# The last two heads' softmax division: the sums carried to the numerators' rows by a 0/1 matmul and inverted there, in place of transposing there and back

## The chip, the cores and the metric

The kernel runs on one core of a Trainium2 chip. The metric is device time in microseconds. Five engines work on it, each in the order of its own queue: TensorE (PE: matmuls, with PEld for its weight loads), VectorE (DVE), ScalarE (ACT), GpSimd (POOL) and SyncE (SP), which issues most DMAs. They wait for each other by semaphores. Matmul results land in PSUM, in eight banks of 128 rows by 512 f32 columns; all else is in SBUF or in DRAM.

## The reference

Two branches share a layer-normalised x (2048 tokens, width 512); their product is added to x:

```
xn = layernorm(x)
q, k, v = split(xn @ wqkv)            # 32 heads of 16
p = softmax(q k^T / 4)                # per head, 2048 x 2048
s = concat_heads(p v) @ wo
h = layernorm(xn)
y = W2 gelu(W1 h + b1) + b2           # over the tokens
out = x + s * silu(y)
```

## The kernel before, in words

**Stages.** First x is normalised and q, k, v are made (to about 147 us). Then one long loop (line 1222) goes over 16 pairs of heads, two spans of 1024 queries for each, and 16 key blocks of 128. For each it computes scores (line 982, 50 rows: 48 of a split q and k, and two rows that subtract the row maximum), the exponential on ACT (line 987), and the values (line 998). Ahead of them the maxima are taken (lines 525 and 529), and the token MLP's matmuls (line 1139) are woven between. When the maxima and the MLP are done, the loop's last part (lines 1273 to 1292) weaves in the output product with wo (lines 1016 to 1024, issued by line 1183, tile dn).

**Values and sums.** The values of a pair of heads go to one PSUM bank of 128 rows by 512 queries, in four strips of 32 rows: head a and query half c make strip 2a + c. v carries 16 columns of ones between the two heads' v, so each strip holds 16 rows of numerators and 16 rows that all equal the softmax sum. For head a = 0 the numerators are rows 0 to 15 of the strip and the sum is row 16; for a = 1 the sum is row 0 and the numerators are rows 16 to 31.

**Division.** `put_away` (line 709) copies the bank to a tile ev. For the first 15 pairs the numerators and sums go to DRAM, are inverted there in a compact shape (line 744: 128 rows of 64 columns) and come back. The last pair has no time for that: `own` (line 812) divides it in SBUF. For each of the two spans:

- `one` transposes ev by 128 columns at a time (line 821: four matmuls with an identity), so that queries are rows and each sum is one column; inverts eight columns twice (line 824); and copies each reciprocal over 32 columns (line 826) to a tile `wide`.
- `two` transposes `wide` back with four f32 matmuls against the identity (line 835, each recorded as two passes), so that every numerator's row has its reciprocal.
- `times` multiplies (line 841, DVE) and makes the upper part of a split number on ACT (line 842); `lower` makes the lower part on DVE (`sub`, line 94).

**Where these run.** The first span's parts are in the list `asides`. In the loop's last part each half-step issues four scores, possibly three matmul items of the output product in two row halves, then one aside (line 1280), then the values that are due. The first span has two asides, `one` and `move_in`; the latter holds `two`, `times`, `lower` and four DMAs on SP that move the 16 numerator rows to their place (line 859). Score tiles and the output product's tiles (dn) take their PSUM banks in turn from one list of seven; the aside's tile takes one from there too.

The second span's parts run after the loop, in the tail (lines 1313 to 1389), which is written out by hand. `some(n)` issues n of 24 matmuls (line 1320) that belong to the last two output blocks and need nothing of the last heads. `product(n)` makes three matmuls (lines 101 to 103) with the last heads' 128 columns k = n // 2: two use the upper part, the third the lower part. `gated`, `added` and `in_parts` (lines 1347 to 1364) multiply a finished block by its gate, add x, and store it. Their DVE work is queued behind that of `times` and `lower`.

Of the kernel before, what the change touches and what calls it, by code (L numbers as in the profile page):

```python
# [8 lines left out]
F32 = mybir.dt.float32  # L9
F32R = mybir.dt.float32r  # L10
AF = mybir.ActivationFunctionType
OP = mybir.AluOpType
# [9 lines left out]
def tile_attention_token_mixer(ctx, tc, x, wqkv, wo, w1, b1, w2, b2, out):  # L22
    nc = tc.nc
    P = 128
    S, D = x.shape
    F = w1.shape[1]
    DH = 16
# [13 lines left out]
    def pool(name, bufs, **kw):  # L41
        return ctx.enter_context(tc.tile_pool(name=name, bufs=bufs, **kw))
# [22 lines left out]
    ps_sc = Banks("ps_sc", 4)  # L65
    ps_mx = Banks("ps_mx", 3)
# [12 lines left out]
    ident = const.tile([P, P], F32, name="ident")  # L79
# [13 lines left out]
    def sub(eng, o, a, b):  # L93
        eng.tensor_tensor(out=o, in0=a, in1=b.bitcast(F32), op=OP.subtract)  # L94

    def move(dst, src, queue=nc.sync):

        queue.dma_start(dst.bitcast(F32), src.bitcast(F32))  # L98
# [7 lines left out]
    qs, ks, vps = {}, {}, {}  # L106
# [63 lines left out]
    with (  # L170
# [15 lines left out]
        for part in range(3):  # L186
            cols = slice(part * D, (part + 1) * D)
# [9 lines left out]
        for n, part in enumerate((2, 0, 1)):  # L197
            for kd in range(ND):
                nm = ("raw", "wh", "wl")[(n * ND + kd) % 3]
# [61 lines left out]
        def first(c, some=range(4)):  # L261
            def dst(b):
                xn[4 * c + b] = px.tile([P, D], F32, name="xn", bufs=8)
                return xn[4 * c + b]

            return Norm(lambda b: xr[4 * c + b], dst, some=some)
# [11 lines left out]
        def bank():  # L278

            i = turn_of[0] = (turn_of[0] + 1) % 8  # L280
            pl, nm = ((ps_sc, "sc"), (ps_mx, "mx"), (ps_av, "av"))[i % 2 if i < 7 else 2]
            return pl.tile([P, 512], F32, name=nm)
# [52 lines left out]
        one, two = first(0, range(2)), first(0, range(2, 4))  # L335
# [65 lines left out]
        for c in range(NC):  # L401
# [20 lines left out]
            for n, (part, g) in enumerate(order):  # L422
                m = slice(g * P, (g + 1) * P)
                begun = c == 0 and part == 0
                ps = pq[g] if begun else bank()
                for w, z in ((wh, 0), (wh, 1), (wl, 0))[begun:]:
                    for kd in range(ND):
                        nc.tensor.matmul(  # L428
                            ps, w[part][:, kd, m], xt[kd][:, z, :],
                            start=w is wh and z == 0 and kd == 0, stop=w is wl and kd == ND - 1,  # L430
# [62 lines left out]
    pp = pool("pp", 18, reuse_waits="tile")  # L493
    sm = pool("sm", 2, reuse_waits="tile")
    el = pool("el", 2, reuse_waits="tile")

    pieces = []
    later = []
# [2 lines left out]
    def after(n, f):  # L501

        later.append(f if n == 1 else lambda: after(n - 1, f))
# [205 lines left out]
    def put_away(p, span, av):  # L709

        ev = el.tile([P, 512], F32, name="ev")
        if p == NP - 1 and span < QH - 1:

            nc.vector.tensor_copy(ev, av)
        else:
            nc.scalar.copy(ev, av)
        if p == NP - 1:
            own(span, ev)
            return
        g, i = divmod(p, 4)  # L720
        if i == 0:
            dens[span] = sm.tile([P, 64], F32, name="d")
        rows = ev.rearrange("(j r) q -> r j q", r=32)
        for a in range(2):
            h = 2 * i + a
            nc.sync.dma_start(
                dens[span][DH * h : DH * (h + 1), :],
                rows[16 - 16 * a, 2 * a : 2 * a + 2, :].rearrange("c (j q) -> c j q", q=64),
            )
        nc.sync.dma_start(num_d[g][span][160 * i : 160 * i + P, :], ev)  # L730
        if i == 3 or p == NP - 2:
            invert(g, span)
# [76 lines left out]
    asides = []  # L809
    own_done = []  # L810

    def own(span, ev):
        rq = sm.tile([P, 4, 4], F32, name="rq", bufs=1)
        wide = el.tile([P, 512], F32, name="t", bufs=4)

        def one(pl=ps_mx, nm="mx", spread=1):

            ps = pl.tile([P, 512], F32, name=nm)
            for k in range(4):
                at = slice(k * P, (k + 1) * P)  # L820
                nc.tensor.transpose(ps[:, at], ev[:, at], ident)
            turned = ps.rearrange("p (k j r) -> p k j r", k=4, j=4)
            for a in range(2):
                nc.vector.reciprocal(rq[:, :, 2 * a : 2 * a + 2], turned[:, :, 2 * a : 2 * a + 2, 16 - 16 * a])
            for k in range(0, 4, 4 // spread):
                nc.vector.tensor_copy(
                    wide.rearrange("p (k j r) -> p k j r", k=4, j=4)[:, k : k + 4 // spread],
                    rq[:, k : k + 4 // spread].unsqueeze(3).to_broadcast([P, 4 // spread, 4, 32]),
                )

        def two(pl=ps_mx, nm="mx", ks=range(4)):

            ps = pl.tile([P, 512], F32, name=nm)
            for k in ks:
                nc.tensor.matmul(
                    ps[:, k * P : (k + 1) * P], wide[:, k * P : (k + 1) * P], ident, start=True, stop=True,
                )
            return ps

        def times(ps, of, at):  # L840
            nc.vector.tensor_tensor(out=ev[:, at], in0=ps[:, at], in1=ev[:, at], op=OP.mult)
            nc.scalar.copy(of[:, 0, at], ev[:, at])

        def lower(of, at):
            sub(nc.vector, of[:, 1, at], ev[:, at], of[:, 0, at])

        if span == QH - 1:
            asides.extend((one, two, times, lower))
            return

        def move_in():
            ps = two()
            of = el.tile([P, 2, 512], F32R, name="uo")
            times(ps, of, slice(0, 512))
            lower(of, slice(0, 512))
            for a in range(2):
                for c in range(2):
                    row = 32 * (2 * a + c) + DH * a
                    move(oc[ND - 1, c][96 + DH * a : 112 + DH * a, :, :], of[row : row + DH, :, :])
            after(4, lambda: own_done.append(True))  # L860

        asides.extend((one, move_in))


    last_w = {}
# [77 lines left out]
    def plan_halves():  # L943

        rows = [oc[g, c][:, m, :].bitcast(F32) for c in range(NC - 1) for g in range(ND - 1) for m in range(2)]
        own = PARTS - NB // 2
        for n in range(own, len(blocks) - 3):
            b = blocks[n]
            in_halves.extend(((ys, b, y_d[b]), (gts, b, g_d[b])))
        in_halves.extend((gates, b, g_d[b]) for b in range(NB // 2, NB))  # L950
        in_halves[:] = [(to, b, row, of) for (to, b, of), row in zip(in_halves, rows, strict=True)]
# [175 lines left out]
    def halves(lead, n):  # L1127


        parts, then = ([], []), []  # L1130

        def each(x, f):
            if f:
                then.append(f)
                return
            ps, w, m, first, last = x
            for a, made in ((lead, parts[0]), (1 - lead, parts[1])):
                r = slice(64 * a, 64 * a + 64)
                made.append(lambda r=r, start=first and a == lead, stop=last and a != lead: nc.tensor.matmul(  # L1139
                    ps, w(r), m(r), start=start, stop=stop,  # L1140
                ))

        take(n, each)
        return *parts, then
# [5 lines left out]
    def count():  # L1150


        left = -done
        for i, n in enumerate(sizes):
            left += n
            if left > 0:
                break
        new_block[0] = left == n
        if left == 9:
            return 4  # L1160
        return min(6, -(-left // -(-3 * left // (15 if i == SLOW else 16)))) if left > 0 else 0
# [60 lines left out]
    for s in range(0, total + 1, 2):  # L1222
# [13 lines left out]
        if s < NU and t >= 0:  # L1236
            steady[0] = True
            one, two, then = halves(lead, count())
# [18 lines left out]
        elif s < NU:  # L1257

            for i in range(4):
# [4 lines left out]
                some = []  # L1264
# [35 lines left out]
        if 0 <= t < NT:  # L1300
            p, r = divmod(t, SPP)
# [13 lines left out]
    for b in range(PARTS, NB):  # L1315
        sums[b] = ps_sc.hold("dn")[0][:, :D]
        for g in range(ND):
            o, at = oc[g, b // 4], slice(b % 4 * P, (b % 4 + 1) * P)
# [5 lines left out]
    def some(n):  # L1324
        for f in beside[:n]:
            f()
        del beside[:n]

    one, two, times, lower = asides
    some(4)  # L1330
    one(ps_sc, "sc", 4)
    some(3)
    shares = [two(ps_sc, "sc", [k]) for k in range(4)]
    some(1)
    of = ks[NP - 1][:, :1024].rearrange("p (a q) -> p a q", a=2)
    half = [NB // 2 + 4 * c + k for k in range(4) for c in range(2)]
# [27 lines left out]
            nc.sync.dma_start(out[b * P : (b + 1) * P, at], to[:, at])  # L1364


    cols = [slice(k * P, (k + 1) * P) for k in range(4)]
    for k in range(5):
        if k < 4:
            times(shares[k], of, cols[k])  # L1370
# [46 lines left out]
```

## Time and profile before

| | |
|---|---|
| median of the runs | 1627.11 us |
| fastest run | 1627.04 us |
| the profiled execution's own time | 1627.03 us |
| its span, first to last instruction | 1625.2 us |
| granted TensorE clock | 1.00 |

In the profile, each row of a timeline has the start in us from the span's beginning, the duration, the engine, the line of the kernel, the operation, out<-in tiles with their shapes, and in brackets how long the engine stood idle before and who released it. Rows that follow each other on one engine and are alike are merged, with their count. Rows of groups have count, busy us, mean ns of one, and idle us before.

### The profile page before, as it was taken

The numbers are of one execution on the slowest core, as the hardware profiler recorded it, in microseconds if no ns is written. First come the engines' busy times: TensorE is split into PE (matmuls) and PEld (weight loads), VectorE is DVE, ScalarE is ACT, GpSimd is POOL, SyncE is SP. The second block draws the span as 40 slices with busy tenths as digits, with TensorE's granted clock in tenths as the row PEclk, the third lists the DMA queues.
The fourth block names the chain that finished last, engine by engine and source line by source line (L and its number), as shares of the span: only waits on it lengthen the run. The fifth ranks groups of instructions, "written<-read, shape, count | busy, mean of one in ns | idle before, by whom it ended". The sixth has DMA issues, their size and how long they took to land.

```text
span 1625.2 us, 31294 instructions
## 1 busy us (share of the span) xinstructions
PE 1618.5 (100%) x11956; PEld 880.1 (54%) x11956; DVE 1422.0 (87%) x2500; ACT 1195.7 (74%) x2313; POOL 559.5 (34%) x663
## 2 busy tenths in 40 slices
PE   9999999999999999999999999999999999999998
PEld 7888854554555544544545545444555455444444
DVE  7655999999999999999999999999999999999956
ACT  3333477777777777778877877777778778888885
POOL 1224844342244432342333332322322224632440
PEclk9999999999999999999999999999999999999999
DMA  7478441515143141826151512314151615453364
GB/s 227 175 248 210 114 94 41 95 41 76 41 70 72 32 80 34 244 67 109 40 86 38 94 56 41 79 23 68 37 86 38 112 39 94 121 102 118 112 203 176
DMA packets 152466, 155.60 MB, mean 96 GB/s; under 512 B 51628, under 2 KB 110252, under 8 KB 149244
## 3 DMA queue, kind: packets, MB, share of 16 engines
q1 hardware_dynamic: 147900, 152.85, 38.6%
q8 instruction: 94, 1.54, 0.4%
q0 software_dynamic: 4416, 0.75, 0.4%
q14 instruction: 56, 0.46, 0.1%
HBM read 101.86 MB, written 50.58 MB: 94 GB/s over the span
## 4 chain that ended last, share of the span: by engine, by line
PE 99%; DVE 1%; ACT 0%; DMA 0%; issue 0%; DVEq 0%
PE av L998 31%; PE dn L1139 25%; PE sc L982 17%; PE mx L525 14%; PE dn L663 3%; PE sc L428 3%; PE mx L428 2%; PE av L428 1%; PE sc L101 0%; PE sc L103 0%; PE sc L102 0%; PE mx L982 0%; PE dn L1320 0%; PE mx L101 0%; PE mx L103 0%; PE mx L102 0%
## 5 line engine op out<-in xcount | busy, mean ns | idle before, releaser
L529 DVE TENSOR_REDUCE mxp<-mx 128x1 f32<-128x512 f32 x2026 | 1250.8, 682 | 117.4 <-PE mx L525 92.2
L987 ACT ACTIVATE prob<-sc 128x512 f32<-128x512 f32 x2004 | 1039.1, 606 | 282.9 <-PE sc L982 127.8
L525 PE MATMUL mx<-big 48*128 48x512 f32 x2026 | 773.0, 418 | 0.0
L982 PE MATMUL sc<-big 50*128 50x512 f32 x2004 | 738.5, 412 | 0.1
L998 PE MATMUL av<-prob,vp 128*32 128x512 f32 x4096 | 545.5, 604 | 0.0
L1139 PE MATMUL dn<-hu,wh 64*128 64x512 f32 x1520 | 508.0, 404 | 0.0
L982 PEld LDWEIGHTS sc<-big 50*128 50x128 f32 x2004 | 354.4, 186 | 234.5 <-ACT prob L987 210.4
L525 PEld LDWEIGHTS mx<-big 48*128 48x128 f32 x2026 | 358.0, 185 | 196.3 <-DVE mxp L529 177.9
L1139 PEld LDWEIGHTS dn<-hu,wh 64*128 64x128 f32 x1520 | 271.7, 184 | 75.2 <-issue 49.5
L1139 PE MATMUL dn<-hu,wl 64*128 64x512 f32 x762 | 302.0, 396 | 0.0
L998 PEld LDWEIGHTS av<-prob,vp 128*32 128x32 f32 x4096 | 80.9, 108 | 178.0 <-issue 166.1
L94 POOL TENSOR_TENSOR wl<-raw,wh 128x512 fp32r<-128x512 f32 x124 | 150.9, 1219 | 60.3 <-ACT wh L166 27.0
L1139 PEld LDWEIGHTS dn<-hu,wl 64*128 64x128 f32 x762 | 140.5, 184 | 13.3
L164 POOL CAST wh<-raw 128x512 fp32r<-128x512 f32 x104 | 60.5, 582 | 189.3 <-PE sc L982 54.4
L552 POOL CAST m<-f 16x128 fp32r<-16x128 f32 x32 | 9.0, 281 | 304.7 <-DVE f L541 304.7
L98 POOL DMA_DIRECT2D big<-m x128 | 66.4, 527 | 2.7 <-PE mx L982 2.7
L613 POOL TENSOR_TENSOR sq<-u 128x512 f32<-128x512 f32 x11 | 11.5, 1042 | 132.7 <-ACT u L607 132.6
L1139 PE MATMUL dn<-wh,hu 64*128 64x512 f32 x168 | 55.0, 392 | 0.0
L700 POOL TENSOR_SCALAR t<-t 128x512 f32<-128x512 f32 x16 | 23.8, 1490 | 83.5 <-ACT t L697 83.5
L428 PE MATMUL sc<-xt,big 128*128 128x512 f32 x184 | 44.5, 390 | 0.0
L94 POOL TENSOR_TENSOR hu<-hx,hu 128x512 fp32r<-128x512 f32 x16 | 20.4, 1296 | 68.5 <-ACT hu L271 68.5
L663 PE MATMUL dn<-hu,wh 64*128 64x512 f32 x128 | 42.3, 391 | 0.0
(231 smaller groups left out, 1216.2 us busy)
## 6 DMA issues: line engine op xcount, KB each, us to landing
raw<-in_B_w_dram SPq DMA_DIRECT2D x104, 256.0 KB
big<-k_d SPq DMA_DIRECT2D x96, 128.0 KB
big<-q_d SPq DMA_DIRECT2D x96, 128.0 KB
q_d<-sg SPq DMA_DIRECT2D x16, 512.0 KB
k_d<-sg SPq DMA_DIRECT2D x16, 512.0 KB
num_d<-ev SPq DMA_DIRECT2D x30, 256.0 KB
u_d<-uo SPq DMA_DIRECT2D x14, 512.0 KB
hu<-u_d SPq DMA_DIRECT2D x14, 512.0 KB
```

The source lines that it names most:

```text
L94: eng.tensor_tensor(out=o, in0=a, in1=b.bitcast(F32), op=OP.subtract)
L98: queue.dma_start(dst.bitcast(F32), src.bitcast(F32))
L164: nc.gpsimd.tensor_copy(whs[n][:, :m, :], raws[n][:, :m, :])
L428: nc.tensor.matmul(ps, w[part][:, kd, m], xt[kd][:, z, :], start=w is wh and z == 0 and kd == 0, stop=w is wl and kd == ND - 1,)
L525: nc.tensor.matmul(ps, q[o : o + 48, r * P : (r + 1) * P], k[o : o + 48, c * 512 : (c + 1) * 512], start=True, stop=True,)
L529: nc.vector.tensor_reduce(mxp[u // 16][:, a, r % 8, c : c + 1], ps, axis=AX.X, op=OP.max)
L663: nc.tensor.matmul(ps, w(slice(0, 64)), m(slice(0, 64)), start=first, stop=last)
L700: nc.gpsimd.tensor_scalar(t, t, 1.0, None, op0=OP.add)
L982: nc.tensor.matmul(ps, ks[p][o : o + 50, kb * P : (kb + 1) * P], qs[p][o : o + 50, at : at + 512], start=True, stop=True,)
L987: nc.scalar.activation(e, ps, AF.Exp, scale=scale)
L998: nc.tensor.matmul(av[32 * j : 32 * j + 32, :], vps[p][:, kb, 16 * a : 16 * a + 32], prob.pop((t, a, c)), start=kb == 0, stop=kb == NB - 1,)
L1139: made.append(lambda r=r, start=first and a == lead, stop=last and a != lead: nc.tensor.matmul(ps, w(r), m(r), start=start, stop=stop,))
```

## The change

A tile `pick` (128 by 128, f32) is made once from the identity by four POOL copies. Its columns 32j to 32j + 31 are all the identity's column of the row that holds strip j's sum, so the matmul of `pick` with ev puts, in all 32 rows of each strip, that strip's sum. `one` and `two` become one function `share`, a single f32 matmul over the columns asked for, with `pick` as weights. The reciprocal is taken in `times`, of all 128 rows and all columns, from PSUM to `wide`. The first span's asides become one (`move_in`). In the tail there are four shares of 128 columns, each in a bank of its own, directly behind `some(4)`; `some(3)` between the transposes is gone, and these three matmuls are issued later by the `some` ahead of block 14.

```
+    pick = sm.tile([P, P], F32, name="pick", bufs=1)
+    for j in range(4):
+        row = 32 * j + (DH if j < 2 else 0)
+        nc.gpsimd.tensor_copy(pick[:, 32 * j : 32 * j + 32], ident[:, row : row + 1].to_broadcast([P, 32]))
...
     def own(span, ev):
-        rq = sm.tile([P, 4, 4], F32, name="rq", bufs=1)
         wide = el.tile([P, 512], F32, name="t", bufs=4)

-        def one(pl=ps_mx, nm="mx", spread=1):
+        def share(pl=ps_mx, nm="mx", at=slice(0, 512)):

             ps = pl.tile([P, 512], F32, name=nm)
-            for k in range(4):
-                at = slice(k * P, (k + 1) * P)
-                nc.tensor.transpose(ps[:, at], ev[:, at], ident)
...
-        def two(pl=ps_mx, nm="mx", ks=range(4)):
-
-            ps = pl.tile([P, 512], F32, name=nm)
-            for k in ks:
-                nc.tensor.matmul(
-                    ps[:, k * P : (k + 1) * P], wide[:, k * P : (k + 1) * P], ident, start=True, stop=True,
-                )
+            nc.tensor.matmul(ps[:, at], pick, ev[:, at], start=True, stop=True)
             return ps

         def times(ps, of, at):
-            nc.vector.tensor_tensor(out=ev[:, at], in0=ps[:, at], in1=ev[:, at], op=OP.mult)
+            nc.vector.reciprocal(wide[:, at], ps[:, at])
+            nc.vector.tensor_tensor(out=ev[:, at], in0=wide[:, at], in1=ev[:, at], op=OP.mult)
             nc.scalar.copy(of[:, 0, at], ev[:, at])
...
         if span == QH - 1:
-            asides.extend((one, two, times, lower))
+            asides.extend((share, times, lower))
             return

         def move_in():
-            ps = two()
+            ps = share()
             of = el.tile([P, 2, 512], F32R, name="uo")
             times(ps, of, slice(0, 512))
             lower(of, slice(0, 512))
...
-        asides.extend((one, move_in))
+        asides.append(move_in)
...
-    one, two, times, lower = asides
+    share, times, lower = asides
+    cols = [slice(k * P, (k + 1) * P) for k in range(4)]
     some(4)
-    one(ps_sc, "sc", 4)
-    some(3)
-    shares = [two(ps_sc, "sc", [k]) for k in range(4)]
+    shares = [share(ps_sc, "sc", at) for at in cols]
     some(1)
```

More of the change, by code (lines that the diff above doesn't have):

```diff
@@ L812, in own @@
     def own(span, ev):
-        rq = sm.tile([P, 4, 4], F32, name="rq", bufs=1)
         wide = el.tile([P, 512], F32, name="t", bufs=4)
-        def one(pl=ps_mx, nm="mx", spread=1):
+        def share(pl=ps_mx, nm="mx", at=slice(0, 512)):
             ps = pl.tile([P, 512], F32, name=nm)
-            for k in range(4):
-                at = slice(k * P, (k + 1) * P)
[L821 to L828, printed above, removed]
-                )
-        def two(pl=ps_mx, nm="mx", ks=range(4)):
-            ps = pl.tile([P, 512], F32, name=nm)
-            for k in ks:
-                nc.tensor.matmul(
-                    ps[:, k * P : (k + 1) * P], wide[:, k * P : (k + 1) * P], ident, start=True, stop=True,
-                )
+            nc.tensor.matmul(ps[:, at], pick, ev[:, at], start=True, stop=True)
             return ps
         def times(ps, of, at):
-            nc.vector.tensor_tensor(out=ev[:, at], in0=ps[:, at], in1=ev[:, at], op=OP.mult)
+            nc.vector.reciprocal(wide[:, at], ps[:, at])
+            nc.vector.tensor_tensor(out=ev[:, at], in0=wide[:, at], in1=ev[:, at], op=OP.mult)
             nc.scalar.copy(of[:, 0, at], ev[:, at])
@@ L1364, in in_parts @@
             nc.sync.dma_start(out[b * P : (b + 1) * P, at], to[:, at])
-    cols = [slice(k * P, (k + 1) * P) for k in range(4)]
     for k in range(5):
```

## The prediction

> **What bounds the kernel now.** I read the page first (span, engines, chain), then the timeline of the two places where the last heads are divided, then the DVE groups by shape for reciprocals.
>
> ```profile
> span 1625.2 us, 31294 instructions
> PE 1618.5 (100%) x11956; PEld 880.1 (54%) x11956; DVE 1422.0 (87%) x2500; ACT 1195.7 (74%) x2313; POOL 559.5 (34%) x663
> PE 99%; DVE 1%; ACT 0%; DMA 0%; issue 0%; DVEq 0%
> ```
>
> TensorE (PE) is the bound throughout: 99% of the chain that ended last, the other 1% being DVE at the very end. So a pass less on PE is worth its pitch, and a new wait of PE is lost whole. The change touches two places: the first span's division, beside scores and values ("the middle"), and the second span's, on the way to the last products ("the tail"). The middle, before:
>
> ```profile
> 1571.04 0.50 PE L982 MATMUL sc<-big 50*128 50x512 f32 x1
> ...
> 1571.20 0.69 DVE L714 COPY ev<-av 128x512 f32<-128x512 f32 x1
> ...
> 1572.04 0.63 PE L821 MATMUL mx<-ident,ev 128*128 128x128 f32 x4 [0.27 <-DVE ev L714]
> ...
> 1572.60 1.07 PE L998 MATMUL av<-prob,vp 128*32 128x512 f32 x8
> ...
> 1573.08 0.62 ACT L987 ACTIVATE prob<-mx 128x512 f32<-128x512 f32 x1
> ...
> 1573.60 0.50 PE L982 MATMUL sc<-big 50*128 50x512 f32 x1
> ...
> 1574.13 1.09 ACT L987 ACTIVATE prob<-sc 128x512 f32<-128x512 f32 x2 [0.43 <-PE dn L1183]
> ...
> 1574.60 0.69 DVE L962 TENSOR_TENSOR sq<-dn,sq 128x512 f32<-128x512 f32 x1 [1.16 <-PE dn L1183]
> ...
> 1574.96 1.16 PE L835 MATMUL mx<-ident,t 128*128 128x128 f32 x8
> ...
> 1576.05 1.07 PE L998 MATMUL av<-prob,vp 128*32 128x512 f32 x8
> ...
> 1576.15 0.69 DVE L841 TENSOR_TENSOR ev<-mx,ev 128x512 f32<-128x512 f32 x1
> 1576.88 0.62 ACT L842 CAST uo<-ev 128x512 fp32r<-128x512 f32 x1 [0.69 <-DVE ev L841]
> ...
> 1577.04 0.50 PE L982 MATMUL sc<-big 50*128 50x512 f32 x1
> ...
> 1577.70 1.06 PE L998 MATMUL av<-prob,vp 128*32 128x512 f32 x8
> ...
> 1578.25 2.53 SPq L98 DMA_DIRECT2D hu<-uo  x4
> ...
> 1578.70 0.50 PE L982 MATMUL sc<-big 50*128 50x512 f32 x1
> ...
> 1581.06 0.50 PE L982 MATMUL sc<-big 50*128 50x512 f32 x1
> ```
>
> The columns are start, duration, engine, line, operation and tiles. The PE rows of scores mark half-steps, which I call H0 (from 1571.04), H1 (1573.60), H2 (1577.04), H3 (1578.70). A half-step has four scores and eight value passes; H1 and H3 have six matmuls of the output product (dn) too. Without an aside a half-step lasts 1.66 (H2: 1578.70 - 1577.04) or 2.36 (H3: 1581.06 - 1578.70). H0 lasts 2.56 and H1 3.44, so the two asides cost PE 0.90 + 1.08 = 1.98 us. ACT is nearly as full: its exponentials follow each other every 0.49 us (two in 1.09 with 0.60 each), eight of them 3.9 us in the 4.02 us of two half-steps, and the values of a half-step need the four exponentials of the half-step before.
>
> **The price on which it hangs** is a reciprocal of 128 or 512 columns, which the kernel before never runs:
>
> ```profile
> L744 DVE RECIPROCAL d<-d 128x64 f32<-128x64 f32 x6 | 3.3, 553 | 0.2
> L239 DVE RECIPROCAL r<-t 128x4 f32<-128x4 f32 x7 | 1.2, 178 | 1.9 <-ACT t L234 1.9
> L239 DVE RECIPROCAL r<-t 128x2 f32<-128x2 f32 x2 | 0.3, 160 | 0.3 <-ACT t L234 0.3
> L824 DVE RECIPROCAL rq<-mx 128x8 f32<-128x8 f32 x2 | 0.3, 182 | 0.8 <-PE mx L821 0.8
> ```
>
> From 4 to 64 columns it grows by (553 - 178)/60 = 6.25 ns a column over 153 ns fixed; 2 columns (165 worked out, 160 seen) fit. The row from PSUM, 8 columns in 182, gives 203 by that line, so a PSUM source is not dearer per column. Estimates: 128 columns 0.95 us, 512 columns 3.35 us. Bounds: all of the 553 in the columns, 8.64 ns each, gives 1.11 and 4.42; below, the multiplications of the same shapes, 0.28 and 0.69, if a long run went at their rate. I take the line, since 64 columns lie nearest to it.
> [...]
>
> **The middle, step by step.** Removed from PE: four transposes and eight passes. Added: one f32 product of 512 columns. Eight value passes, which are four strips of such a product side by side, take 1.00 (1577.70 to the next PE row, 1578.70), eight passes over 128 columns 1.09 (1574.96 to 1576.05); I take 1.0. It starts at 1572.04 as the transposes did (it waits for the same copy, L714), so it ends at 1573.04 where the transposes let the values start at 1572.60: 0.44 later. H1 then has no aside (1.08 gone): H2 would start at 1576.40 and not 1577.04, 0.64 us gained, if nothing waited.
> But it waits. The two asides are now one, so the upper part's copy stands on ACT behind H0's four exponentials and ahead of H1's four. DVE: product seen at about 1573.15 (transposes 1572.67 to reciprocal 1572.71 shows the gap), reciprocal to 1576.50, multiplication 0.69 to 1577.23, ACT's copy 0.62 to 1577.89. H1's exponentials, which ran from 1574.13, start about 1577.77 (0.5 behind the copy's start) and end at 1578.37, 1578.86, 1579.33, 1579.82. ACT had been free since 1573.70 (1573.08 + 0.62).
> PE meanwhile goes through H1 (its values need only H0's exponentials) to 1576.40. H2's first score takes the bank that the reciprocal read: 1576.55. The second and third take banks of H1's first and second scores: 1578.4 and 1578.9. The fourth takes the bank of the dn block whose evacuation (L962, before at 1574.60) is now queued on DVE behind the reciprocal, the multiplication and the lower part, which itself waits for the copy: lower part 1577.93 to 1578.62, evacuation to about 1579.25, score at 1579.3. H2's values end with the strip that needs the fourth exponential: 1579.86 + 1.0 = about 1580.8. H3 started at 1578.70 before, so the middle costs **+2.1 us** net. H2's exponentials end by 1581.75, H3's values want them at 1582.2: no further wait. PE is full from there, so none of the 2.1 comes back.
> On SP the four moves of uo (1578.25 before, about 1578.65 after) now stand ahead of four loads that were issued before them. These loads' tiles are used by later output blocks, 10 us on; cost nothing, at most the 2.5 us that the moves take to issue, if that cover were gone.
>
> **The tail, step by step,** in the clock of before, the 2.1 left out:
>
> ```profile
> 1608.68 0.60 PE L821 MATMUL sc<-ident,ev 128*128 128x128 f32 x4
> ...
> 1609.32 0.28 DVE L824 RECIPROCAL rq<-sc 128x8 f32<-128x8 f32 x2 [2.94 <-PE sc L821]
> ...
> 1609.91 1.16 PE L835 MATMUL sc<-ident,t 128*128 128x128 f32 x8
> 1610.51 0.49 DVE L841 TENSOR_TENSOR ev<-sc,ev 128x128 f32<-128x128 f32 x2 [0.24 <-PE sc L835]
> ...
> 1610.84 0.30 ACT L842 CAST big<-ev 128x128 fp32r<-128x128 f32 x1 [2.49 <-DVE ev L841]
> ...
> 1611.19 0.51 PE L101 MATMUL sc<-uo,big 128*128 128x512 f32 x1
> ...
> 1612.63 1.28 DVE L1351 TENSOR_TENSOR prob<-sc,hu 128x512 f32<-128x512 f32 x2
> ...
> 1614.43 1.49 DVE L1355 TENSOR_TENSOR prob<-big,prob 128x512 f32<-128x512 f32 x2
> ...
> 1615.85 1.87 DVE L1351 TENSOR_TENSOR prob<-sc,hu 128x512 f32<-128x512 f32 x3
> ...
> 1617.64 1.47 DVE L1355 TENSOR_TENSOR prob<-big,prob 128x512 f32<-128x512 f32 x2
> ...
> 1619.04 0.68 DVE L1351 TENSOR_TENSOR prob<-dn,hu 128x512 f32<-128x512 f32 x1
> ...
> 1619.75 0.69 DVE L1355 TENSOR_TENSOR prob<-big,prob 128x512 f32<-128x512 f32 x1
> ...
> 1620.30 0.39 PE L103 MATMUL dn<-uo,big 128*128 128x512 f32 x1
> 1620.73 0.42 DVE L1362 TENSOR_TENSOR prob<-dn,hu 128x256 f32<-128x256 f32 x1 [0.29 <-PE dn L103]
> ```
>
> PE: the four share products start at 1608.68 (0.27 each, the rate of L835: 1.09 for four), one dn matmul follows, to 1610.0. The first reciprocal starts at 1609.28 (L835 to L841 shows 0.60 from first pass to reader). DVE then runs, for each of four columns, reciprocal 0.95 + 0.04, multiplication and lower part at 0.21 each (the pitch of L841's pair): reciprocals start at 1609.28, 1610.48, 1611.89, 1613.30, the last lower part about 1614.95. DVE comes to its first gating at 1615.17; before, at 1612.63.
> PE's first product wants ACT's copy (1610.85): 1610.9, 0.3 earlier than 1611.19, but its third matmul wants the first lower part, which stands on DVE behind two reciprocals: 1611.96, a wait of 0.6. Three dn matmuls that filled the gap before stand later, so 43 matmuls follow against 40 before, at 0.2336 (39 pitches from 1611.19 to 1620.30): the last starts at 1621.3 and not 1620.30. **PE alone: +1.0.**
> DVE's work behind the lower parts takes, by the starts above, 1.80 for three gatings, 1.42 for two sums (1614.43 to 1615.85), 1.79, 1.40, 0.71, and 0.65 for the last sum: 7.8 us with no wait left in it. 1615.17 + 7.8 = 1622.95 for L1362, at 1620.73 before; PE is done by then. **The tail costs +2.2**: DVE is the bound there, and PE's +1.0 lies beside it.
>
> **The mask.** Four POOL copies to fill pick wait for a late matmul of the V product:
>
> ```profile
> 145.90 0.39 PE L103 MATMUL mx<-wvh,xt 128*128 128x512 f32 x1
> ...
> 148.20 1.28 POOL L94 TENSOR_TENSOR wl<-raw,wh 128x512 fp32r<-128x512 f32 x1 [4.35 <-ACT wh L166]
> ...
> L552 POOL CAST m<-f 16x128 fp32r<-16x128 f32 x32 | 9.0, 281 | 304.7 <-DVE f L541 304.7
> ```
>
> That matmul ends at 146.29. The smallest POOL cast seen takes 0.28, so four copies end by about 147.4; POOL waits for ACT until 148.20. Nothing, or up to 1 us if they took longer, held up the weight split, and the first blocks wanted it.
>
> **Sum.** 2.1 + 2.2 = +4.3 us. The profiled execution took 1627.03 us (span 1625.2, 1.8 around it), the median shown is 1627.11: 1627.1 + 4.3 = **1631.4 us**.
>
> **Rivals.**
> - *The reciprocal is dearer:* 8.64 ns a column. Middle +1.07 more, tail 4 x 0.15 more: +6.0, 1633.1. The fixed time of the short reciprocals speaks against it. [...]
> - *The middle's wait is absorbed,* because another strip order or a spare bank lets PE run on: only the tail, and between -0.64 and 0 in the middle: 1628.7 to 1629.3. For it: ACT stood 0.69 for L841 before and PE lost nothing. Against: 3.6 us is more than a half-step of 2.0.
> - *Not slower:* a long reciprocal runs at the rate of other DVE work (0.69 and 0.28). Then the copy ends near 1575.2, H2 waits only some 0.15, middle about -0.5; in the tail the first product starts at 1610.25 without a gap: -0.24. 1626.4. It decides where 512 columns take under some 1.3 us; the 553 for 64 columns is against it.
>
> **Numbers.** Forecast 60%, dearer reciprocal 14%, middle absorbed 14%, not slower 7%, something else 5%. The forecast's own range is 1630.2 to 1632.6 (the f32 product between 0.9 and 1.1, the waits 0.5 either way). With the two neighbours the range is 1628.4 to 1634.0. All cases lie within 2%, about what a measurement of this kernel can tell from no change (1594.6 to 1659.7): same 98%; slower by over 2% 1.5%, faster 0.5%, both only through something not seen here.
>
> **What would show it.** L826 in the changed kernel: reciprocals of 128x512 near 3.35 us and of 128x128 near 0.95. ACT's copy after a gap of 3.5 us behind H0's exponentials; H2 about 4 us long in place of 1.66. In the tail, DVE without idle from the first reciprocal to the last block and PE done before it. I am wrong if the 128x512 reciprocal is under 2 us, or if PE's half-steps show no stretch.

## The result, and the profile after

The changed kernel takes 1633.22 us (median of 6 runs, 1631.15 to 1634.63); the kernel before takes 1627.06 beside it (6 runs). One of these six took 3885.2 us, the other five 1626.84 to 1627.11. The ratio is 1.0036 with the 95% interval [1.0025, 1.0047]: 6.2 us slower, within 2%, with an interval that excludes no change. The forecast was +4.3 (1631.4). The sign, the two places and the price of each held; a third loss of some 1.5 to 1.7 us was not in the sum.

The profiled run of the changed kernel took 1632.96 us, with a span of 1631.1; the span before was 1625.2. The unseen price comes first. These are the reciprocals of the changed kernel in the groups by shape (count, busy us, mean ns of one, idle before):

```profile
L826 DVE RECIPROCAL t<-sc 128x128 f32<-128x128 f32 x4 | 3.8, 952 | 2.7 <-PE sc L822 2.7
L826 DVE RECIPROCAL t<-mx 128x512 f32<-128x512 f32 x1 | 3.4, 3357 | 1.3 <-PE mx L822 1.3
L748 DVE RECIPROCAL d<-d 128x64 f32<-128x64 f32 x6 | 3.3, 553 | 0.2
```

The line through 4 and 64 columns gave 0.95 and 3.35 us; 952 and 3357 ns were measured. The upper bound of 8.64 ns a column, 1.11 and 4.42 us, isn't borne out: the two rows differ by 2405 ns over 384 columns, 6.26 ns each.

Now the middle of the changed kernel, in the timeline (start, duration, engine, line, operation and tiles, and in brackets the idle time before and its releaser). H0 starts at 1571.20 here:

```profile
1571.20 0.50 PE L968 MATMUL sc<-big 50*128 50x512 f32 x1
...
1572.20 1.10 PE L822 MATMUL mx<-ev,pick 128*128 128x512 f32 x2 [0.27 <-DVE ev L718]
...
1573.33 3.36 DVE L826 RECIPROCAL t<-mx 128x512 f32<-128x512 f32 x1 [1.28 <-PE mx L822]
...
1574.79 0.40 PE L1169 MATMUL dn<-wh,hu 64*128 64x512 f32 x2
...
1576.72 0.69 DVE L827 TENSOR_TENSOR ev<-t,ev 128x512 f32<-128x512 f32 x1
1576.74 0.50 PE L968 MATMUL sc<-big 50*128 50x512 f32 x1
1577.45 0.62 ACT L828 CAST uo<-ev 128x512 fp32r<-128x512 f32 x1 [3.59 <-DVE ev L827]
1577.97 1.08 ACT L973 ACTIVATE prob<-sc 128x512 f32<-128x512 f32 x2
1578.10 0.69 DVE L94 TENSOR_TENSOR uo<-ev,uo 128x512 fp32r<-128x512 f32 x1 [0.68 <-ACT uo L828]
1578.62 0.50 PE L968 MATMUL mx<-big 50*128 50x512 f32 x1 [1.37 <-ACT prob L973]
1578.71 0.69 DVE L948 TENSOR_TENSOR sq<-dn,sq 128x512 f32<-128x512 f32 x1
...
1579.88 1.39 PE L984 MATMUL av<-prob,vp 128*32 128x512 f32 x8
...
1581.20 0.79 PE L968 MATMUL sc<-big 50*128 50x512 f32 x1
...
1582.22 0.63 PE L1169 MATMUL dn<-wh,hu 64*128 64x512 f32 x2
...
1583.63 1.36 PE L984 MATMUL av<-prob,vp 128*32 128x512 f32 x8
...
1584.91 0.50 PE L968 MATMUL sc<-big 50*128 50x512 f32 x1
```

The reader is to see three things. ACT stood idle for 3.59 us, until the multiplication gave it its copy, and H1's exponentials start only behind that copy (1577.97). PE, after one score of H2 at 1576.74, stands for 1.37 until the first of them has freed a bank. And from about 1580.9 on PE's own rows are longer: eight value passes take 1.39 and 1.36 where they took 1.06 (the 1.39 is in part a wait, as an experiment below shows), and the dn matmuls of 1582.22 take 0.63, with the next 0.42 behind them, where those of H1 (1574.79) took 0.40 with the next 0.23 behind. The longer dn matmuls are no wait: it is the clock. The windows show it (busy us of PE, PEld, DVE, ACT and POOL with their counts, then the granted clock, the DMA share and GB/s), before first and the changed kernel second:

```profile
1576.00:1586.00 10.00, 10.00 (x76) 3.88 (x75) 4.18 (x7) 9.19 (x19) 0.00 (x0) 1.00 0.63 176
```

```profile
1576.00:1586.00 10.00, 8.54 (x46) 3.16 (x42) 4.75 (x7) 7.20 (x14) 0.00 (x0) 0.83 0.48 134
```

A granted clock of 0.83 over 10 us is 1.7 us of full clock lost. In windows of 0.25 us it is 1.00 up to 1580.75, 0.73 in the next, 0.50 from 1581.00 to 1584.25, 0.95 in the next and then 1.00 again: half the clock for 3.4 us, from about 1580.87 to 1584.28. From H0 to the half-step behind H3 it takes 13.71 us (1571.20 to 1584.91), where it took 10.02 (1571.04 to 1581.06): +3.7, of which at most 1.7 is the clock, so that at least 2.0 is the wait.

The tail of the changed kernel:

```profile
1611.51 0.50 PE L1306 MATMUL dn<-wh,hu 128*128 128x512 f32 x1
...
1612.96 0.96 DVE L826 RECIPROCAL t<-sc 128x128 f32<-128x128 f32 x1 [2.71 <-PE sc L822]
...
1614.70 0.50 PE L101 MATMUL sc<-uo,big 128*128 128x512 f32 x1 [0.87 <-ACT big L828]
...
1615.76 0.50 PE L103 MATMUL sc<-uo,big 128*128 128x512 f32 x1 [0.33 <-DVE big L94]
...
1618.66 0.29 DVE L94 TENSOR_TENSOR big<-ev,big 128x128 fp32r<-128x128 f32 x1 [0.16 <-ACT big L828]
```

```profile
1624.97 0.39 PE L103 MATMUL dn<-uo,big 128*128 128x512 f32 x1
```

```profile
1626.58 0.41 DVE L1347 TENSOR_TENSOR prob<-dn,hu 128x256 f32<-128x256 f32 x1
```

I measure the tail from the first of the `some(4)` matmuls (1611.51; 1607.65 before) to the last block's multiplication (L1347 here, L1362 before). It takes 15.07 us; before it took 13.08 (1607.65 to 1620.73): +2.0. From the reciprocal on DVE has one gap, of 0.16. L1347 has no bracket: it waited for nobody, while its like before waited 0.29 for PE. PE's last matmul starts 13.46 behind the first, before 12.65: +0.8, beside DVE's time as forecast.

### The profile page after: what moved, and what is told of

It reads as the page before. It is cut to its first block, busy times and chain, and to the rows that moved or that the text cites. A ratio compares the mean times of both kernels' runs of the same rounds, so it can differ in the third digit from the quotient of the medians.

```text
span 1631.1 us, 31263 instructions
## 1 busy us (share of the span) xinstructions
PE 1620.9 (99%) x11942; PEld 880.4 (54%) x11942; DVE 1427.0 (87%) x2496; ACT 1196.0 (73%) x2313; POOL 559.7 (34%) x667
## 4 chain that ended last, share of the span: by engine, by line
PE 98%; DVE 1%; ACT 0%; issue 0%; DMA 0%; POOL 0%; DVEq 0%; POOLq 0%
PE av L984 31%; PE dn L1125 24%; PE sc L968 16%; PE mx L529 14%; PE sc L428 3%; PE dn L667 2%; PE mx L428 2%; PE av L428 1%; PE mx L332 0%; PE sc L103 0%; PE sc L101 0%; PE sc L102 0%; PE dn L1169 0%; PE dn L668 0%; PE mx L103 0%; PE mx L101 0%
```

## The experiments

The theory: DVE's reciprocal delays two chains of the middle (about +2.0), PE's wait there lets the granted clock fall (about +1.7, not forecast), and DVE sets the end of the tail (+2.0). Against it stand the rivals that the reciprocal isn't the cause at all but the new order of the asides, that the slow rows come from the matmul with `pick` and not from the wait, and that the tail's loss is PE's. The kernels have other line numbers; tiles and operations tell the rows. Times are medians, with the kernel before on the same chip.

**One part at a time.** The middle changed and the tail as before:

```
-    share, times, lower = asides
+    one, two, times, lower = asides
...
-    shares = [share(ps_sc, "sc", at) for at in cols]
+    one(ps_sc, "sc", 4)
+    some(3)
+    shares = [two(ps_sc, "sc", [k]) for k in range(4)]
```

> The first span is divided as in the changed kernel, the second span as before. Theory (the reciprocal's columns cost the time; the middle and the tail add up; the wait in the middle also drops TensorE's clock): about +2.2 us with a clock of 1.000 and up to +5.7 where the clock drops after the wait, so 1629.3 to 1632.8, with a spread of some us between runs. Rival (the clock drop has nothing to do with the middle): 1629.3 in every run, clock 1.000. Rival (the middle's wait is given back later): 1627.

And the tail changed, with the middle as before:

```
         def move_in():
-            ps = share()
+            ps = two()
...
-            times(ps, of, slice(0, 512))
+            times_back(ps, of, slice(0, 512))
...
-        asides.append(move_in)
+        asides.extend((one, move_in))
```

> The first span is divided as before, the second span as in the changed kernel. Theory: +2.0 us, 1629.1, no spread, clock 1.000 in every run, because no PE wait is long enough here to move the clock. Rival (the clock drop comes with the change as a whole, or at random): a spread of some us as in the changed kernel. Rival (PE, not DVE, bounds the tail): +0.8, 1627.9.

Before took 1626.75. The middle alone took 1630.56 (+3.8, ratio 1.0024 [1.0014, 1.0033]), from 1628.83 to 1631.50; the tail alone 1628.85 (+2.1, ratio 1.0014 [1.0004, 1.0024]). The fastest run of the middle alone, with a granted clock of 1.000 over the run, is 2.1 above before. Its profiled run (clock 0.998) again has slow PE rows, between 1579.76 and 1583.52, and 0.83 granted over 1576 to 1586. The tail alone has 1.00 there, its runs lie between 1628.03 and 1629.63, about as wide as those of before (1626.19 to 1628.16), and their clocks are 0.999 or 1.000, as those of before are. So the fall belongs to the middle.

**Is it the reciprocal?** The same order of work with a copy in its place, which leaves the inversion out (the numerators are multiplied by the sums):

```
-            nc.vector.reciprocal(wide[:, at], ps[:, at])
+            nc.vector.tensor_copy(wide[:, at], ps[:, at])
```

> The changed kernel with copies in place of its five wide reciprocals, so that the inversion is left out and the numerators are multiplied by the sums. Theory (it is the reciprocal's 6.25 ns a column): a copy takes 0.69 or 0.28 us, nothing waits long, the PE work saved shows: 1626.4, clock 1.000. Rival (the order of the queues costs the time, whatever stands in the reciprocal's place): 1629 or more.

It took 1626.14 (-0.6, ratio 0.9998 [0.9988, 1.0007], not clear of noise).

```profile
1574.80 0.69 DVE L826 COPY t<-mx 128x512 f32<-128x512 f32 x1 [1.28 <-PE mx L822]
```

The copy takes 0.69 for 512 columns, and H3 starts 7.20 after H0 (1572.66 to 1579.86) against 7.66 before: -0.46. The clock is 1.00 over 1576 to 1586 with the same matmul with `pick` in place, so that matmul doesn't make the slow rows. The share matmul and the single aside cost nothing by themselves: in this order of work the whole loss comes with the reciprocal's length. It is also the rival "not slower" run as a kernel: -0.5 in the middle and 1626.4 were worked out for it.

**Is it the wait that lowers the clock?** The changed kernel, with 20 transposes of the identity put ahead of H2's first score, where PE has next to nothing to do:

```
+        if filler[0] == 1:
+            for _ in range(20):
+                nc.tensor.transpose(ps[:, :P], ident, ident)
+            filler[0] = 0
```

> The changed kernel with 20 transposes of the identity ahead of the first score that waits in the middle, about 1.8 us of work inside the 2 us wait; their results are overwritten. Theory (the wait itself lets TensorE's clock fall, and that is the rest of the loss): clock 1.000 in every run, time 1631.2 without the spread of the changed kernel (1631.15 to 1634.63). Rival (the clock has another cause): the same spread, median 1633; and where the filler does not fit into the wait, up to 1.8 us more.

Its PE rows:

```profile
1571.53 0.50 PE L974 MATMUL sc<-big 50*128 50x512 f32 x1
...
1577.08 2.40 PE L972 MATMUL sc<-ident 128*128 128x128 f32 x20
1579.41 0.50 PE L974 MATMUL sc<-big 50*128 50x512 f32 x1
...
1580.22 1.25 PE L990 MATMUL av<-prob,vp 128*32 128x512 f32 x8
...
1581.40 0.50 PE L974 MATMUL sc<-big 50*128 50x512 f32 x1
...
1582.77 1.07 PE L990 MATMUL av<-prob,vp 128*32 128x512 f32 x8
1583.77 0.50 PE L974 MATMUL sc<-big 50*128 50x512 f32 x1
```

With more work on PE it is faster: 1631.18 (7 runs, 1630.31 to 1631.81), +4.4 beside its own runs of before (ratio 1.0027 [1.0016, 1.0038]), where the changed kernel was +6.2 beside its own. Its clocks are 0.999 or 1.000 in all runs. From H0 (1571.53) to the half-step behind H3 it takes 12.24, +2.2 over before and 1.5 less than the changed kernel; H3's values take 1.07, and the windows show 1.00 over 1576 to 1586. The transposes take 2.33 and not the 1.8 expected, but they delay nothing: H2's values start 8.69 behind H0, in the changed kernel 8.68 (1579.88). So the wait is as long as ever, but filled, and the fall is gone. Held at full clock, the 3.7 of the middle split into 2.2 for the wait and 1.5 for the clock. That is less than the 1.7 of lost clock, for H2's values take 1.25 here too: part of their 1.39 in the changed kernel was not the clock's. What the spread of the changed kernel is made of fits: its fastest run, 1631.15, had a clock of 1.000 over the run and lies 4.1 above before; the other five had 0.997 or 0.998 and took 1632.29 to 1634.63. There is a trace of the profiled run alone, so that the fall is missing in the fastest is inferred from its clock.

**Which chain does PE wait for?** Three versions of the middle, tail as before, and the changed kernel again beside them. In the changed kernel ACT's copy delays the exponentials, and the dn evacuation (DVE reading a finished dn block out of its PSUM bank, which frees the bank for a score) is queued on DVE behind the lower part. First, the copy moved to POOL, so that ACT is free:

```
-            times(ps, of, slice(0, 512))
+            nc.vector.reciprocal(wide, ps)
+            nc.vector.tensor_tensor(out=ev, in0=wide, in1=ev, op=OP.mult)
+            nc.gpsimd.tensor_copy(of[:, 0, :], ev)
```

> The middle as changed, the tail as before; in the middle the upper part's copy runs on POOL, so ACT's exponentials no longer stand behind it, while on DVE the lower part still stands ahead of the dn block's evacuation. Theory (two chains of about the same length, over ACT and over DVE, end the same wait): the fourth score still waits for the evacuation, some 1.8 us net in place of 2.2: only 0.3 to 0.4 us better than middle only. Rival (it is ACT's queue alone): the whole wait goes, 1626.5.

Second, ACT's copy left where it was, and the lower part and the moves put into one aside later, so that DVE's queue is free for the evacuation:

```
+        def divide_it():
+            ps = share()
+            now_of.append(el.tile([P, 2, 512], F32R, name="uo"))
+            times(ps, now_of[0], slice(0, 512))
+
         def move_in():
-            ps = share()
-            of = el.tile([P, 2, 512], F32R, name="uo")
-            times(ps, of, slice(0, 512))
+            of = now_of[0]
             lower(of, slice(0, 512))
...
-        asides.append(move_in)
+        asides.extend((divide_it, move_in))
```

> The middle as changed, the tail as before; in the middle the lower part and the moves come one aside later, so that the dn block's evacuation stands ahead of the lower part on DVE, while ACT's copy stays where it was. Theory (two chains): H2's second score still waits for the first exponential behind the copy, 2.1 to 2.2 us net, no gain against middle only. Rival (it is DVE's queue alone): the wait goes, 1627 or less.

Third, both: the first aside is the share and the reciprocal, the second the multiplication, with both parts on POOL:

```
+        def invert_it():
+            nc.vector.reciprocal(wide, share())
+
         def move_in():
-            ps = share()
...
-            times(ps, of, slice(0, 512))
-            lower(of, slice(0, 512))
+            nc.vector.tensor_tensor(out=ev, in0=wide, in1=ev, op=OP.mult)
+            nc.gpsimd.tensor_copy(of[:, 0, :], ev)
+            sub(nc.gpsimd, of[:, 1, :], ev, of[:, 0, :])
...
-        asides.append(move_in)
+        asides.extend((invert_it, move_in))
```

> The middle's first aside is the sums' matmul and the reciprocal alone; the multiplication comes one aside later, and both parts are made on POOL; the tail as before. Both queues are freed, the reciprocal is the same 3.36 us. Theory: the evacuation waits only for the reciprocal (some 0.3 us on H2's fourth score), ACT for nothing, the PE work saved shows: -0.2 to -0.4 against before, 1626.5, clock 1.000. Rival (DVE held for 3.4 us costs by itself): 1628 or more.

> The changed kernel once more, on the chip of the runs beside it. Theory (the middle +2.2, the tail +2.0, the clock's fall 0 to 3.5): 1631 to 1634.6 with a spread of over 2 us, on a chip whose runs of before are at 1626.8.

Before took 1627.43 here. The changed kernel took 1634.12 (4 runs, ratio 1.0039 [1.0024, 1.0054]). These medians hold the clock's fall too, where a run has it. ACT freed alone took 1630.56 (+3.1, ratio 1.0018 [1.0008, 1.0027]), DVE's queue freed alone 1630.85 (+3.4, 1.0020 [1.0010, 1.0029]), both 1627.17 (-0.3, 0.9998 [0.9989, 1.0008], no difference clear of noise). The rows say why one is not enough. With ACT free:

```profile
1577.70 0.50 PE L1000 MATMUL sc<-big 50*128 50x512 f32 x1
...
1579.08 0.69 DVE L94 TENSOR_TENSOR uo<-ev,uo 128x512 fp32r<-128x512 f32 x1 [0.71 <-POOL uo L872]
...
1579.69 0.69 DVE L980 TENSOR_TENSOR sq<-dn,sq 128x512 f32<-128x512 f32 x1
...
1580.43 0.56 PE L1000 MATMUL mx<-big 50*128 50x512 f32 x1 [2.00 <-DVE sq L980]
```

three scores of H2 go at once, and the fourth waits 2.00 us for the bank of the dn block, whose evacuation stands on DVE behind the lower part. With DVE's queue free:

```profile
1577.60 0.69 DVE L983 TENSOR_TENSOR sq<-dn,sq 128x512 f32<-128x512 f32 x1
1577.72 0.62 ACT L858 CAST uo<-ev 128x512 fp32r<-128x512 f32 x1 [3.60 <-DVE ev L857]
1578.24 1.08 ACT L1008 ACTIVATE prob<-sc 128x512 f32<-128x512 f32 x2
...
1578.88 0.49 PE L1003 MATMUL mx<-big 50*128 50x512 f32 x1 [1.37 <-ACT prob L1008]
```

the evacuation comes early, and PE stands for ACT as it did. With either wait the clock is 0.83 over 1576 to 1586. With both freed:

```profile
1573.32 3.36 DVE L868 RECIPROCAL t<-mx 128x512 f32<-128x512 f32 x1 [1.28 <-PE mx L852]
...
1576.60 0.63 DVE L981 TENSOR_TENSOR sq<-dn,sq 128x512 f32<-128x512 f32 x1
...
1577.28 0.49 PE L1001 MATMUL mx<-big 50*128 50x512 f32 x1
...
1578.70 0.49 PE L1001 MATMUL sc<-big 50*128 50x512 f32 x1
```

the same 3.36 us reciprocal runs, the fourth score comes 0.54 after the first (1576.74), and H3 starts 7.51 behind H0 (1571.19), 0.15 sooner than before, at a clock of 1.00. The matmul with `pick` is in it too. Here the long reciprocal costs nothing by its length; in the changed kernel it costs by what was queued behind it.

**The tail: DVE or PE?** With the middle as before, the tail's lower parts were moved to POOL, and then each reciprocal of the tail taken twice:

```
-            sub(nc.vector, of[:, 1, at], ev[:, at], of[:, 0, at])
+            sub(nc.gpsimd if span == QH - 1 else nc.vector, of[:, 1, at], ev[:, at], of[:, 0, at])
```

> As the run with only the tail changed (the middle is that of before), and the four lower parts of the tail are made by POOL, not by DVE. Theory (DVE without idle sets the end, PE's later end lies beside it): DVE loses four times 0.21 us, so the tail costs +2.1 - 0.84 = about +1.3, about 1628.0 beside 1626.7; the last block's multiplication still has no wait for PE ahead of it. POOL's subtraction of 128 columns should take about 0.35 (it took 1.29 for 512 columns beside 0.69 on DVE), so the first product's third matmul waits less than 0.33. Rival (the tail's cost is PE's: the wait of 0.33 for the first lower part, the 0.87 ahead of the first product, and three matmuls that stand later): the end follows PE, which gains only the wait, so +1.8 to +2.1 is left.

```
             nc.vector.reciprocal(wide[:, at], ps[:, at])
+            nc.vector.reciprocal(wide[:, at], ps[:, at])
```

> As the run with only the tail changed (the middle is that of before), and each of the tail's four reciprocals is taken twice. Theory: DVE runs without idle, so four more of 0.95 + 0.04 come straight on top: +2.1 + 4.0 = about +6.1, about 1632.8 beside 1626.7, and DVE shows no idle time from the first reciprocal to the last block. Rival (PE sets the end): only what stands ahead of the first product counts: one reciprocal more ahead of the first upper part, two ahead of the first lower part, so +2.1 + 1.0 to 2.0 = +3.1 to +4.1, with idle time on DVE ahead of the last block.

Before took 1626.87. Lower parts on POOL: 1627.72 (+0.9, ratio 1.0006 [0.9997, 1.0016], not clear of noise, +1.3 expected); reciprocals twice: 1632.75 (+5.9, ratio 1.0037 [1.0023, 1.0051]). The traces are sharper than the medians. The last block's multiplication, in the one and in the other, waits for nobody:

```profile
1621.05 0.42 DVE L1377 TENSOR_TENSOR prob<-dn,hu 128x256 f32<-128x256 f32 x1
```

```profile
1626.47 0.42 DVE L1378 TENSOR_TENSOR prob<-dn,hu 128x256 f32<-128x256 f32 x1
```

From the first `some(4)` matmul to the last block's multiplication the first takes 14.04 (1607.01 to 1621.05) and the second 19.03 (1607.44 to 1626.47), against 13.08 before and 15.09 with the tail alone (1607.16 to 1622.25). Taking 4 x 0.21 and the gap of 0.17 from DVE shortens the tail by 1.05, and adding 4 x 0.99 lengthens it by 3.94: DVE sets it. One POOL subtraction took 0.45, not the 0.35 I had expected, and that cost nothing.

The doubled tail shows the clock a second time (the last row is of the windows):

```profile
1611.62 0.50 PE L101 MATMUL sc<-uo,big 128*128 128x512 f32 x1 [1.86 <-ACT big L859]
1611.96 0.39 PE L102 MATMUL sc<-uo,big 128*128 128x512 f32 x1
1613.68 0.80 PE L103 MATMUL sc<-uo,big 128*128 128x512 f32 x1 [1.33 <-DVE big L94]
1614.27 0.63 PE L101 MATMUL sc<-uo,big 128*128 128x512 f32 x1
```

```profile
1611.00:1617.00 6.00, 4.05 (x10) 2.97 (x11) 5.83 (x11) 0.89 (x3) 0.00 (x0) 0.63 0.00 0
```

After the wait of 1.86 and two matmuls the clock falls, and in the slow stretch comes the second wait, of 1.33. The matmuls' rows go to 0.63 each (0.39 at full clock), as long as those at 0.50 in the middle, until about 1619.4. A clock of 0.63 over these 6 us is 2.2 us of full clock lost, or 4.4 us at 0.50: by this estimate the fall starts at about 1612.6 and lasts 6.8 us. There it costs little: DVE, not PE, ends the tail.

## Why the prediction came out as it did

- *The reciprocal's price* was the hinge and was right to 10 ns, by a straight line over eight times the longest row seen. The total alone would have misled: 1633.2 is what the rival of the dearer reciprocal gave (1633.1). Its row, 3357 ns and not 4.42 us, rules it out.
- *The middle's wait* was right in its chain and its size: +2.1 forecast, +2.2 measured with the wait filled, at least 2.0 in the changed kernel. The price of the share (1.0) held: it starts at 1572.20 and the values follow at 1573.23. The two waits named, for the exponentials and for the evacuation, are each nearly enough alone, as the two half-cures show. The rivals that the wait is absorbed and that the change is not slower fell.
- *The step that failed* is the end of that part: "no further wait. PE is full from there, so none of the 2.1 comes back". No wait followed, but PE's durations were taken from rows at a clock of 1.00, and the clock was not held constant by anything: the stretch of waiting lowered it. H3 was to take 2.36; it took 3.71 (1581.20 to 1584.91). The missing term is 1.5 us (13.71 less 12.24, the same stretch with the wait filled), in five of the six runs by their clocks, and the forecast's own range (to 1632.6) had no place for it. That 1633.2 lies inside the whole range is luck: only the allowance for a dearer reciprocal reaches so far.
- *The tail:* +2.2 forecast, +2.0 measured, with DVE as the bound and PE's share beside it (+1.0 forecast, +0.8 measured). Two steps came out within 0.1 on PE: its first product starts 3.19 behind the first of the `some(4)` matmuls (3.25 forecast), the third matmul, which waits for the lower part, 4.25 (4.31). On DVE the first reciprocal starts 1.45 behind and not 1.63, which is most of the 0.2.
- *At nothing:* the four copies to `pick` ran on POOL from 145.61 to 146.27, sooner and shorter than the 147.4 reckoned, while POOL's next work started at 148.13. SP's loads behind the moves (from 1581.39) released no wait of PE.

The terms measured in the profiled run are 3.7 for the middle, the clock's fall in it, and 2.0 for the tail: 5.7 of the 5.9 by which the spans differ; H0 also starts 0.16 later (1571.20 against 1571.04), ahead of the change's first work there.

What stays open: how much idle time, spread in what way, lowers the clock, and why the fall is missing in a run now and then. One stretch of 1.37 without a matmul did it in the changed kernel, with one score in the half microsecond before; one of 2.00 did it with ACT free; the two waits of the tail (0.87 and 0.33) left the clock at 1.00. PE's busy time alone doesn't tell them apart: it was busy for 2.2 us of the 3.4 us, the fall's own length, ahead of the fall in the changed kernel (1577.45 to 1580.86), and for 2.2 of the 3.4 us about the tail's waits (1613.40 to 1616.81), at 1.00.

## What to carry to other kernels

A long instruction on an engine with time to spare is paid by what is queued behind it and by who waits for that: before such an edit, list for each engine what stands behind, and give every chain its own engine or a later place; curing one of two equal chains gained little (+3.1 and +3.4 us with one freed, +3.8 with neither, -0.3 with both, each beside its own runs of before). Where TensorE is the bound, a new wait of it can cost more than its length (here 3.7 us for 2.2): look at the granted clock of the stretch after it, and at the runs' spread. And check a total against the row of each term, since a wrong rival can give the right sum.

## What the runs showed of the hardware

- *The granted clock fell to 0.50 after a stretch with gaps.* In the middle of the changed kernel PE ran one score, stood 1.4 us and went on; 2.2 us later the granted clock went to 0.50 and its matmuls followed at 0.43 and not 0.23. Windows of 0.25 us give 3.4 us at 0.50 there (about 1580.87 to 1584.28). In each of the five traces with the fall in the middle (the changed kernel in both its traces, the middle alone, ACT freed, DVE's queue freed) the clock is 0.83 over 1576 to 1586, which at 0.50 is some 3.4 us; the doubled tail's 6.8 is the estimate above. The changed kernel's slow stretch starts 2.2 us behind the end of the wait; with ACT freed the row right behind the wait (1580.43) is long already, 0.56 for 0.50. PE was not idle ahead of the fall: in the changed kernel it was busy for 2.2 of the 3.4 us before it.
- *Matmuls with no use saved time here:* with 20 transposes in the wait the clock was 1.00 over 1576 to 1586 (0.83 without), and the middle took 12.24 us and not 13.71, 1.5 less.
- *The reciprocal on DVE* cost 6.25 ns a column over some 153 fixed: 178 ns for 4 columns and 553 for 64, read from SBUF, 952 for 128 and 3357 for 512, read from PSUM; 8 columns from PSUM took 182, where that line gives 203. A copy of 512 columns from PSUM took 0.69 us, a fifth of the reciprocal.
